# Convolution pieces woven into an attention kernel: two free streams over all chunks in place of streams in pairs

## The chip, the cores and the metric

The kernel runs on one core of a Trainium2 chip. The core has a matrix engine (TensorE, PE in the rows), a vector engine (VectorE, DVE), an activation engine (ScalarE, ACT), a general engine (GpSimd, POOL) and an engine that issues most transfers (SyncE, SP). Each engine takes its instructions strictly in the order in which the program lists them and waits on semaphores for the others. The metric is the time of one execution in microseconds (us); lower is better. Three runs of the kernel before took 1151.06 to 1153.36 us.

## The reference

Two independent computations share the launch. Their results stand side by side in the output.

```python
# A: a long convolution, 2048 positions, 576 channels, 128 states per channel
P = exp(dt * A[:, :, None] * l)                   # A, B, C complex
K = einsum("dn,dnl,dn->dl", C, P, dt * B).real    # kernel of the convolution
y = irfft(rfft(u, 2L) * rfft(K, 2L))[:L] + u * Dskip
# B: attention, 2048 positions, 32 query heads of 18, one shared key and value head
q = x @ wq ; k = x @ wk ; v = x @ wv
p = softmax(q k^T * 18 ** -0.5)
out = (p v) @ wo
return concatenate([y, out])
```

## The kernel before

**Attention.** Keys lie on partitions, so a score tile is 128 keys by 2 heads by 512 queries. There are 1,024 of them. For each, PE makes two matmuls (`s`, L516), ACT one exponential into a tile `P` (L527), and PE multiplies by the values into the bank `ops` (L823; one product takes the `P` of two score tiles, 512 products in all). Score tiles have three buffers in PSUM. The order is written in rounds (L835): a round writes the scores of three tiles, then fills PE until a score buffer is free again with products and with pieces of other work. There are 342 rounds. Every 16 products DVE copies `ops` to `o` (L534), and PE may write the one `ops` bank again only after that copy. Beside it run the query projections (`q`), bounds on the scores (`up`) and the output projection (`op`, 40 pieces of four matmuls for each 512 queries). What is left of the last output projection is done after the last product, in `finish` (L625, tiles `fin`).

**Convolution.** 576 channels are worked on in 12 chunks of 48. A chunk has a `front` (L1264): DVE makes powers of the states' exponentials (`factors`, rows `t`, `fr`, `sum`, `dif`) and two tables (`tables`, rows `tab`, `tt`), from which PE makes the kernel (`kg`, four banks a chunk, copied by DVE to `ksb`); it then goes through DRAM into the tile `kt`. Its `back` (L1337): PE transforms the input `u` (banks `hu`, `lu`, evacuated by DVE into `scu`) and the kernel (`hk`, `lk` into `sck`), DVE multiplies (`ks`, `acc`, `pt`, `sv`, `w`), and PE transforms back (`iy`). At chunks 0, 1, 5 and 9 `powers` makes the exponentials and sines for the chunks up to the next of these, a burst: ACT loads another table, does two sines, and loads the exponential's table again. A stream that comes to the burst yields "b" (L1124) and is let go once 8 units of attention's own PE work wait beside it or 16 steps have passed.

All of these pieces on PE (`kg`, `hu`, `lu`, `hk`, `lk`, `iy`, `q`, `up`, `op`) share one PSUM bank (`bank`, L221): the next can begin only when DVE has evacuated the one before.

**What sets the order.** The program is written by a planner in Python with a running guess of when each engine is free (`Clock`). Work other than scores and products lies in generators (`Stream`) that yield "p" before a piece for PE, "v" before a piece for DVE, "w" to wait. `Conv.go` (L1448) advances one conv stream by one piece whenever `fill` (L785) asks; among streams that can go it takes the one that has had the least vector work. `RATE` and `PACE` tie the conv's vector work to the steps of attention (a step is one product): while the conv is behind `PACE` per step, attention's side pieces stand back (L796). `turn` (L1439) puts the streams up in pairs: `back(k)` beside `front(k + 1)`, and the next pair only when both have ended. `meanwhile` (L1287) puts conv vector rows in front of an evacuation while the guess says that the vector engine would stand idle.

```python
if self.n < NCK and not any(st.live for st in self.streams):
    self.n += 1
    self.streams = [Stream(self.back(k, self.kt), self.k)]
    if k + 1 < NCK:
        self.streams.append(Stream(self.front(k + 1), self.k))
```

Of the kernel before, what the change touches and what calls it, by code (L numbers as in the profile page):

```python
# [47 lines left out]
PACE = 1.79  # L48
# [4 lines left out]
GAP = 0.4  # L53
DEFER = 0.5
# [9 lines left out]
NCK = D // ND  # L64
# [918 lines left out]
class Conv:  # L983
# [21 lines left out]
    def setup(self):  # L1005
        nc, cp, a = self.nc, self.cp, self.a
        self.raw, self.stored = {}, 0.0
        self.ut, self.ut_ready, self.kt = {}, [0.0, 0.0], None
        self.dft = cp.tile([P, 2048], F32, name="dft_sb")
        self.pos = cp.tile([P, 2, NB], F32, name="pos_sb")  # L1010
        self.hp = cp.tile([P, 1], F32, name="hp_sb")
        nc.vector.memset(self.hp, HALF_PI)
# [251 lines left out]
    def front(self, k):  # L1264
# [20 lines left out]
        self.kt, self.kt_ready = kt, self.k.t + 9.0  # L1285
# [51 lines left out]
    def back(self, k, kt):  # L1337
# [7 lines left out]
        tt(us[:, 0:4, :], us[:, 4:8, :], us[:, 8:12, :], op=ALU.add)  # L1345
        ks = p1.tile([P, 12, NE], F32, tag="ks", name=f"ks{k}")
# [73 lines left out]
    def early(self):  # L1420
        nc = self.nc
        nc.scalar.dma_start(self.pos, self.a["pos"])
        self.load_burst(0)
        self.load(0)
        self.n, self.burst = -1, False
        self.streams = [Stream(self.front(0), self.k)]
# [12 lines left out]
    def turn(self):  # L1439

        if self.n < NCK and not any(st.live for st in self.streams):
            self.n += 1
            k = self.n
            self.streams = [Stream(self.back(k, self.kt), self.k)] if k < NCK else []
            if k + 1 < NCK:
                self.streams.append(Stream(self.front(k + 1), self.k))

    def go(self, step, credit, lock):  # L1448
        self.turn()
# [4 lines left out]
        for st in self.streams:  # L1454

            if st.kind == "b":
                if st.asked < 0:
                    st.asked = step
                if self.beside() >= 8 or step > st.asked + 16 or self.n < 0:
                    st.kind, st.asked = "v", -1  # L1460
        for st in sorted(self.streams, key=lambda st: (not st.holds, st.work)):
            w0, st.ahead = self.k.work, ahead
            if st.go(step, credit, lock):
                self.work += self.k.work - w0
# [6 lines left out]
    def drain(self):  # L1471
        while self.streams:
            for st in sorted(self.streams, key=lambda st: (not st.holds, st.work)):
# [3 lines left out]
            self.turn()  # L1477
# [98 lines left out]
```

## Time and profile before

| what | value |
|---|---|
| median of 3 runs | 1151.15 us |
| lowest, highest run | 1151.06, 1153.36 us |
| profiled execution, first to last instruction | 1153.0 us |
| PE busy | 1083.5 us, 94% |
| ACT busy | 998.8 us, 87% |
| DVE busy | 987.4 us, 86% |
| POOL busy | 140.6 us, 12% |
| granted TensorE clock, mean | 0.99 |

The profile is one execution. No time of it is known beside its span, which lies between the lowest and the highest run. Busy time of PE counts modelled ends of matmuls that overlap, so 94% is not 94% of what PE could do. In the rows each single-precision matmul shows as two records, so that "x16" of a piece such as `lu` are 8 matmuls, and a piece of four matmuls is "x8". In the order below the count is of matmuls.

### The profile page before, as it was taken

How to read it: one execution, taken by the hardware profiler on the slowest of the kernel's cores; microseconds unless marked ns; L12 is line 12 of the kernel's file. 1: busy time of each engine (PE TensorE's matmuls, PEld its weight loads, DVE VectorE, ACT ScalarE, POOL GpSimd, SP SyncE). 2: the span in 40 equal slices, each digit the busy share in tenths (PEclk: the TensorE clock that was granted, in tenths of full speed). 3: DMA queues.
4: the chain of work that ended last, by engine and by line, in shares of the span. 5: the costliest groups of instructions: out<-in, count | busy, mean ns of one | idle time of the engine just before them, and what ended most of it. 6: DMA issues, size and time to landing. Idle time of an engine off the chain costs nothing.

```text
span 1153.0 us, 33012 instructions
## 1 busy us (share of the span) xinstructions
PE 1083.5 (94%) x13886; PEld 395.9 (34%) x13886; DVE 987.4 (86%) x1679; ACT 998.8 (87%) x1052; POOL 140.6 (12%) x257
## 2 busy tenths in 40 slices
PE   6999899989999999989999999999998999999998
PEld 2333233333333334323333333333332333332423
DVE  3697997998997897897799899898699799799694
ACT  2888979879989898998998899988999988899891
POOL 5232320112032000001021200001040000000000
PEclk9899999999999999999999999999999999999999
DMA  7422242114122202112222300202221301301201
GB/s 224 130 57 84 76 133 89 45 41 135 32 67 78 74 29 88 45 63 93 82 79 71 110 21 28 93 28 85 75 78 46 111 20 39 106 19 54 77 33 58
DMA packets 59279, 83.37 MB, mean 72 GB/s; under 512 B 14867, under 2 KB 35335, under 8 KB 58613
## 3 DMA queue, kind: packets, MB, share of 16 engines
q1 hardware_dynamic: 47557, 73.24, 19.4%
q0 software_dynamic: 10848, 7.37, 2.6%
q8 instruction: 111, 1.82, 0.6%
q10 hardware_dynamic: 720, 0.58, 0.2%
q14 instruction: 43, 0.35, 0.1%
HBM read 46.59 MB, written 33.85 MB: 70 GB/s over the span
## 4 chain that ended last, share of the span: by engine, by line
PE 64%; DVE 15%; ACT 14%; issue 5%; DMA 1%; SPq 0%; ACTq 0%; DVEq 0%
PE ops L823 27%; PE s L516 17%; ACT P L527 12%; PE op L193 5%; PE q L408 3%; DVE tab L119 3%; PE kg L1257 3%; PE iy L193 3%; DVE ks L119 1%; DVE acc L119 1%; DVE t L119 1%; PE hk L193 1%; PE fin L193 1%; PE lk L193 1%; DMA xr<-xT 1%
## 5 line engine op out<-in xcount | busy, mean ns | idle before, releaser
L527 ACT ACTIVATE P<-s 128x1024 f32<-128x1024 f32 x992 | 934.8, 1034 | 104.6 <-PE s L516 102.2
L823 PE MATMUL ops<-P,v_sb 128*32 128x512 f32 x4096 | 513.0, 601 | 8.5 <-DVE o L123 8.4
L516 PE MATMUL s<-aug,kaug 55*128 55x512 f16 x2048 | 309.9, 384 | 36.6 <-ACT P L527 30.7
L516 PEld LDWEIGHTS <-kaug 55*128 55x128 f16 x2048 | 92.2, 94 | 371.7 <-issue 328.5
L823 PEld LDWEIGHTS ops<-P,v_sb 128*32 128x32 f32 x4096 | 117.2, 110 | 162.6 <-issue 126.1
L458 POOL DMA_DIRECT2D qd<-qh x116 | 65.7, 573 | 323.2 <-DVE qh L127 320.6
L408 PE MATMUL q<-x,wq_sb 128*32 128x256 f32 x1360 | 84.2, 382 | 3.2 <-DVE sck L119 2.5
L193 PE MATMUL op<-wo_sb,oT 126*32 126x288 f32 (+1 forms) x1048 | 74.8, 410 | 2.6 <-DVE sck L119 1.2
L119 DVE TENSOR_TENSOR tab<-tab,tt 128x576 f32<-128x576 f32 (+1 forms) x72 | 59.1, 821 | 1.4
L123 DVE COPY ksb<-kg 128x192 f32<-128x192 f32 x48 | 17.5, 364 | 49.1 <-PE kg L1257 48.9
L119 DVE TENSOR_TENSOR tt<-fr,sum 128x576 f32<-128x576 f32 (+1 forms) x72 | 58.9, 818 | 0.0
L119 DVE TENSOR_TENSOR tab<-tab 128x576 f32<-128x576 f32 (+1 forms) x72 | 58.9, 818 | 0.0
L119 DVE TENSOR_TENSOR tab<-fr,dif 128x576 f32<-128x576 f32 (+1 forms) x72 | 58.9, 818 | 0.0
L119 DVE TENSOR_TENSOR tab<-sum,fr 128x576 f32<-128x576 f32 (+1 forms) x72 | 58.8, 816 | 0.0
L408 PEld LDWEIGHTS q<-x,wq_sb 128*32 128x32 f32 x1360 | 40.5, 110 | 43.4 <-issue 19.1
L1168 POOL MEMSET fr<- 128x192 f32 x24 | 9.8, 494 | 323.8 <-DVE tt L119 225.2
L119 DVE TENSOR_TENSOR acc<-acc,pt 128x1728 f32<-128x1728 f32 (+2 forms) x36 | 48.7, 1352 | 0.3
L119 DVE TENSOR_TENSOR pt<-us,ks 128x1728 f32<-128x1728 f32 (+2 forms) x36 | 48.2, 1351 | 0.0
L525 ACT ACTIVATE P<-s,bias 128x1024 f32<-128x1024 f32 x32 | 32.7, 1131 | 15.1 <-PE s L516 15.1
L193 PEld LDWEIGHTS op<-wo_sb,oT 126*32 126x32 f32 (+1 forms) x1048 | 29.8, 110 | 42.2 <-issue 17.4
L1257 PEld LDWEIGHTS kg<-tab 128*32 128x32 f32 x2304 | 35.5, 110 | 22.9 <-issue 7.9
L1257 PE MATMUL kg<-tab 128*32 128x64 f32 x2304 | 41.8, 221 | 1.5 <-DVE ksb L123 1.1
(160 smaller groups left out, 1018.0 us busy)
## 6 DMA issues: line engine op xcount, KB each, us to landing
od<-o SPq DMA_DIRECT2D x31, 256.0 KB
aug<-qd SPq DMA_DIRECT2D x124, 55.0 KB
u<-u SPq DMA_DIRECT2D x12, 384.0 KB
kd<-ksb SPq DMA_DIRECT2D x12, 384.0 KB
kt<-kd SPq DMA_DIRECT2D x48, 96.0 KB
outa<-u SPq DMA_DIRECT2D x12, 384.0 KB
pw<-pw SPq DMA_DIRECT2D x8, 528.0 KB
oT<-od SPq DMA_DIRECT2D x16, 252.0 KB
```

The source lines that it names most:

```text
L119: return self.v.tensor_tensor(out, *a, **k)
L123: return self.v.tensor_copy(out, *a, **k)
L193: nc.tensor.matmul(ps[j:e], w[:, j:e], x, start=start, stop=stop, tile_position=(0, j))
L408: nc.tensor.matmul(ps[o, 256 * f:256 * f + 256], w[:, k, i], xt[:, k, x], start=(k == 0), stop=(k == 4), tile_position=(0, 32 * j))
L458: q.dma_start(qd[h:h + n, row + d:row + d + nd, cs], src[i1:i1 + n * nd, :cs.stop - cs.start])
L516: nc.tensor.matmul(ps[:, j, :], self.kaug[r, kb * P:(kb + 1) * P], t[r, :], start=True, stop=True)
L525: nc.scalar.activation(pt, ps, AF.Exp, bias=self.bias, scale=SCALE / QQ)
L527: nc.scalar.activation(pt, ps, AF.Exp, scale=SCALE / QQ)
L823: nc.tensor.matmul(o_ps[32 * j:32 * j + 32, :], self.v[:, kb, :], pts[2 * n + j // 2][:, j % 2, :], start=(kb == 0), stop=(kb == 15), tile ...
L1168: nc.gpsimd.memset(t[:, :, 0:NF:8], one)
L1257: nc.tensor.matmul(ps[32 * g:32 * g + 32, d, :], t[:, :32], t[:, 32:], start=(j == 0), stop=(j == 1), tile_position=(0, 32 * g))
```

## The change

The pairs go. One stream runs all 12 fronts, another all 12 backs. `begun` holds the last chunk whose kernel has been sent to `kt`. A back of chunk 0 waits for kernel 0; a back of chunk k may begin, with the transform of its input, once kernel k - 1 has been sent (`LAG`), and waits before the transform of its kernel until kernel k has been sent. A front waits with its store into `kt` until the back before it has read the tile, as it did. Among streams whose next piece is a vector piece, `go` now takes the stream that had the last vector piece (`on`) first. `PACE` falls from 1.79 to 1.75. The burst's test looks at `begun`. No arithmetic changes.

```diff
-PACE = 1.79
+PACE = 1.75
...
+LAG = (0, -1)
...
-        self.kt, self.kt_ready = kt, self.k.t + 9.0
+        self.kt, self.kt_ready, self.begun = kt, self.k.t + 9.0, k
...
-    def back(self, k, kt):
+    def back(self, k):
...
         yield from self.transform(lambda r: ut[:, r, :], us[:, 4:12, :], f"u{k}", self.ut_ready[k % 2])
         yield "v", 0.0, False
         tt(us[:, 0:4, :], us[:, 4:8, :], us[:, 8:12, :], op=ALU.add)
+        while self.begun < k:
+            yield "w", 0.0, False
+        kt = self.kt
         ks = p1.tile([P, 12, NE], F32, tag="ks", name=f"ks{k}")
...
-        self.n, self.burst = -1, False
-        self.streams = [Stream(self.front(0), self.k)]
+        self.burst, self.on = False, None
+        self.streams = [Stream(self.fronts(), self.k), Stream(self.backs(), self.k)]
+
+    def fronts(self):
+        for k in range(NCK):
+            yield from self.front(k)
+
+    def backs(self):
+        for k in range(NCK):
+            while self.begun < LAG[k > 0] + k:
+                yield "w", 0.0, False
+            yield from self.back(k)
...
-    def turn(self):
-
-        if self.n < NCK and not any(st.live for st in self.streams):
-            self.n += 1
-            k = self.n
-            self.streams = [Stream(self.back(k, self.kt), self.k)] if k < NCK else []
-            if k + 1 < NCK:
-                self.streams.append(Stream(self.front(k + 1), self.k))
-
     def go(self, step, credit, lock):
-        self.turn()
...
-                if self.beside() >= 8 or step > st.asked + 16 or self.n < 0:
+                if self.beside() >= 8 or step > st.asked + 16 or self.begun < 0:
                     st.kind, st.asked = "v", -1
-        for st in sorted(self.streams, key=lambda st: (not st.holds, st.work)):
+        for st in sorted(self.streams, key=lambda st: (not st.holds, st.kind == "v" and st is not self.on, st.work)):
             w0, st.ahead = self.k.work, ahead
+            kind = st.kind
             if st.go(step, credit, lock):
+                if kind == "v":
+                    self.on = st
                 self.work += self.k.work - w0
                 return True
```

Line numbers of the kernel after are higher by one from L54 on (by more behind the changed functions). Three places show how the order moves.

DVE at the transform of the input of chunk 9 (`scu9`), before. `fr10`, `t1_10` and `t2_10` belong to the front of chunk 10.

```order
L123 COPY scu9_11647<-hu90_11663 128x384
L123 COPY fr10_11677<-pw_10_11557 128x48x4 x2
L123 COPY fr10_11677<-pw_10_11557 128x48x3
L123 COPY fr10_11677<-pw_10_11557 128x48x4 x2
L123 COPY fr10_11677<-pw_10_11557 128x48x3
L119 TENSOR_TENSOR t1_10_11691<-pw_10_11557 128x48x4
L119 TENSOR_TENSOR t2_10_11692<-pw_10_11557 128x48x4
L119 TENSOR_TENSOR fr10_11677<-t1_10_11691,t2_10_11692 128x48x4
L119 TENSOR_TENSOR t1_10_11691<-pw_10_11557 128x48x4
L119 TENSOR_TENSOR t2_10_11692<-pw_10_11557 128x48x4
L119 TENSOR_TENSOR fr10_11677<-t1_10_11691,t2_10_11692 128x48x4
L119 TENSOR_TENSOR scu9_11647<-lu90_11686,scu9_11647 128x384
```

The same place after. `stage3` is a burst's row, of the front.

```order
L124 COPY scu9_11036<-hu90_11037 128x384
L120 TENSOR_TENSOR scu9_11036<-lu90_11047,scu9_11036 128x384
L120 TENSOR_TENSOR scu9_11036<-lu90_11047,scu9_11036 128x2x192
L120 TENSOR_TENSOR stage3_10387<-stage3_10387,m3_10388 128x792 x2
L124 COPY scu9_11036<-hu91_11064 128x384
L120 TENSOR_TENSOR stage3_10387<-stage3_10387,m3_10388 128x792 x2
L120 TENSOR_TENSOR scu9_11036<-lu91_11094,scu9_11036 128x384 x2
```

Ten lines (twelve instructions) of the other stream stood between the copy of `hu90` and the first row that frees `lu90`. None stands there now, and two rows of the front stand on either side of the copy of `hu91`.

DVE where the first table of chunk 7 is done (`tab7_0`) and its kernel bank is copied (`ksb7`), before; `acc6` and `ks6` belong to the back of chunk 6.

```order
L119 TENSOR_TENSOR tab7_0_8582<-tab7_0_8582 128x24x24
L119 TENSOR_TENSOR tab7_0_8582<-tab7_0_8582,tt7_0_8_4_8838 128x24x24
L119 TENSOR_TENSOR acc6_8697<-acc6_8697,pt6_2_8850 128x96x6
L119 TENSOR_TENSOR acc6_8697<-acc6_8697 128x768
L123 COPY ksb7_8581<-kg7_0_0_8921 128x4x16x3
```

The same place after.

```order
L120 TENSOR_TENSOR tab7_0_8420<-tab7_0_8420 128x24x24
L120 TENSOR_TENSOR tab7_0_8420<-tab7_0_8420,tt7_0_8_4_8572 128x24x24
L120 TENSOR_TENSOR ks6_8219<-sck6_8220 128x2x192 x4
L124 COPY ks6_8219<-ks6_8219 128x32x6
L120 TENSOR_TENSOR ks6_8219<-ks6_8219 128x32x18
L124 COPY ksb7_8419<-kg7_0_0_8643 128x4x16x3
```

Two rows of the back stood between the last table row and the copy; six stand there now (one line is four rows).

PE at the end, before: from the last matmul of the last score tile (`s3_15_15`) over both halves of the last transform back (`iy110`, `iy111`) and the last products (`ops3_7`) to the first tiles of `finish` (`fin0`, `fin1`) and its broadcast `bc`.

```order
L516 MATMUL s3_15_15_14227<-aug3_113,kaug_109 128x512
L193 MATMUL iy110_14232<-w11_14162,dft_sb_98 32x192 x16
L823 MATMUL ops3_7_13960<-P3_14_14_14203,v_sb_115 32x512 x2
L823 MATMUL ops3_7_13960<-P3_15_14_14205,v_sb_115 32x512 x2
L823 MATMUL ops3_7_13960<-P3_14_15_14207,v_sb_115 32x512 x2
L823 MATMUL ops3_7_13960<-P3_15_15_14230,v_sb_115 32x512 x2
L193 MATMUL iy111_14258<-w11_14162,dft_sb_98 32x192 x16
L193 MATMUL fin0_14281<-wo_sb_107,oT3_13187 32x288 x16
L193 MATMUL fin1_14282<-wo_sb_107,oT3_13187 32x288 x8
L669 MATMUL bc_14280<-rc_last_14279,b4_13989 128x256
```

The same place after.

```order
L517 MATMUL s3_15_15_14277<-aug3_113,kaug_109 128x512
L194 MATMUL iy111_14282<-w11_14169,dft_sb_98 32x192 x16
L824 MATMUL ops3_7_14001<-P3_14_13_14222,v_sb_115 32x512 x2
L824 MATMUL ops3_7_14001<-P3_15_13_14224,v_sb_115 32x512 x2
L824 MATMUL ops3_7_14001<-P3_14_14_14249,v_sb_115 32x512 x2
L824 MATMUL ops3_7_14001<-P3_15_14_14251,v_sb_115 32x512 x2
L824 MATMUL ops3_7_14001<-P3_14_15_14253,v_sb_115 32x512 x2
L824 MATMUL ops3_7_14001<-P3_15_15_14280,v_sb_115 32x512 x2
L194 MATMUL fin0_14317<-wo_sb_107,oT3_13146 32x288 x12
L194 MATMUL fin1_14318<-wo_sb_107,oT3_13146 32x288 x8
L670 MATMUL bc_14316<-rc_last_14315,b4_13974 128x256
```

The first half (`iy110`) has moved ahead of the last score tile, the second half ahead of the last three products, and 20 matmuls of `fin` come before `bc` where there were 24. Over the whole of `finish` there are 92 where there were 116: six pieces of the output projection moved into the rounds, which hold 131 of them before and 137 after.

## Rows read from the trace of the kernel before


**Rows 1.** the page, parts 1 and 4: busy us (share) xinstructions; the chain by engine

```profile
PE 1083.5 (94%) x13886; PEld 395.9 (34%) x13886; DVE 987.4 (86%) x1679; ACT 998.8 (87%) x1052; POOL 140.6 (12%) x257
...
PE 64%; DVE 15%; ACT 14%; issue 5%; DMA 1%; SPq 0%; ACTq 0%; DVEq 0%
```

**Rows 2.** the view of waits: engine, line, waited for: us in total, times, longest

```profile
ACT P L527 <- PE s L516: 102.2, 186, 2.4
...
DVE ksb L123 <- PE kg L1257: 48.9, 33, 2.9
PE s L516 <- ACT P L527: 30.7, 81, 2.0
...
PEld lu L193 <- DVE scu L123: 11.0, 16, 1.1
...
PEld kg L1257 <- DVE ksb L123: 7.1, 11, 1.1
```

**Rows 3.** timeline of PE, 917 to 932 us: start us, us, engine line op, [idle before]

```profile
918.24 0.86 PE L193 MATMUL lu<-u,dft_sb 128*32 128x192 f32 x16
...
930.88 1.18 PE L193 MATMUL op<-wo_sb,oT 126*32 126x288 f32 x16 [0.81 <-DVE scu L119]
```

**Rows 4.** timeline of DVE, the same stretch

```profile
919.09 0.61 DVE L119 TENSOR_TENSOR t<-pw 128x192 f32<-128x192 f32 x2
919.74 0.52 DVE L119 TENSOR_TENSOR fr<-t,t 128x192 f32<-128x192 f32 x1
...
921.31 1.01 DVE L119 TENSOR_TENSOR scu<-lu,scu 128x384 f32<-128x384 f32 x2
...
929.71 1.02 DVE L119 TENSOR_TENSOR scu<-lu,scu 128x384 f32<-128x384 f32 x2
```

**Rows 5.** groups by line: form xcount | busy us, mean ns of one | idle before

```profile
L119 DVE TENSOR_TENSOR t<-pw 128x192 f32<-128x192 f32 x36 | 11.2, 355 | 0.3
```

**Rows 6.** timeline of all engines, 118 to 147 us, the first burst

```profile
132.42 1.28 ACT L1125 ACT_TABLE_LOAD   x1
...
133.06 4.09 PE L408 MATMUL q<-x,wq_sb 128*32 128x256 f32 x72
...
137.64 1.28 ACT L527 ACT_TABLE_LOAD   x1
...
140.01 0.60 PE L516 MATMUL s<-aug,kaug 55*128 55x512 f16 x2 [2.00 <-ACT P L527]
```

**Rows 7.** timeline of all engines, 244 to 262 us

```profile
250.92 0.69 DVE L123 COPY o<-ops 128x512 f32<-128x512 f32 x1
...
251.66 1.07 PE L823 MATMUL ops<-P,v_sb 128*32 128x512 f32 x8 [2.26 <-DVE o L123]
```

**Rows 8.** table of windows; PEclk is the granted clock, 1 is 2.4 GHz

```profile
140.00:146.00 6.00, 5.37 (x24) 0.94 (x25) 6.00 (x9) 4.54 (x5) 2.41 (x6) 0.51 0.45 141
146.00:150.00 4.00, 3.23 (x34) 0.82 (x30) 3.83 (x15) 2.85 (x3) 0.91 (x3) 0.89 0.93 265
...
250.00:254.00 4.00, 2.34 (x14) 0.43 (x14) 4.00 (x6) 1.58 (x3) 2.69 (x5) 0.84 0.45 126
254.00:258.00 4.00, 4.00 (x70) 1.61 (x70) 2.59 (x5) 2.21 (x3) 0.00 (x0) 0.73 0.25 85
```

**Rows 9.** timeline of PE from 1126 us to the end

```profile
1126.76 0.39 PE L516 MATMUL s<-aug,kaug 55*128 55x512 f16 x2
...
1130.12 1.48 PE L193 MATMUL iy<-w,dft_sb 128*32 128x192 f32 x32
1131.41 3.10 PE L193 MATMUL fin<-wo_sb,oT 126*32 126x288 f32 x48
...
1135.14 4.57 PE L193 MATMUL fin<-wo_sb,oT 126*32 126x288 f32 x72
...
1145.26 2.15 PE L193 MATMUL fin<-w,o_last 128*32 128x288 f32 x32
```

**Rows 10.** timeline of ACT, 1120 to 1153 us

```profile
1121.18 5.61 ACT L527 ACTIVATE P<-s 128x1024 f32<-128x1024 f32 x6 [0.46 <-PE s L516]
```

More of the change, by code (lines that the diff above doesn't have):

```diff
@@ L1006, in setup @@
         nc, cp, a = self.nc, self.cp, self.a
-        self.raw, self.stored = {}, 0.0
+        self.raw, self.stored, self.begun = {}, 0.0, -1
         self.ut, self.ut_ready, self.kt = {}, [0.0, 0.0], None
@@ L1471, in drain @@
     def drain(self):
-        while self.streams:
-            for st in sorted(self.streams, key=lambda st: (not st.holds, st.work)):
+        while any(st.live for st in self.streams):
+            for st in sorted(self.streams, key=lambda st: (not st.holds, st.kind == "w", st.work)):
                 if st.live:
@@ L1476, in drain @@
                     break
-            self.turn()
 def build(tc, **aps):
```

## The prediction

> **What bounds the kernel now.** I read the page first. PE is busy for 1083.5 us of the 1153.0 us span, ACT for 998.8, DVE for 987.4, and the chain that ended last runs over PE for 64%, DVE for 15% and ACT for 14% [rows 1]. The reader is to see that no engine has much to spare, and that PE leads. The view of waits comes next. ACT waits for scores from PE for 102.2 us in 186 places of at most 2.4 us each, and PE waits for ACT to free a score buffer for 30.7 us [rows 2]. So the loop of 342 rounds is a hand-over between these two, with PE late more often than ACT. What the change moves is work of the third engine, DVE. It can reach the time only where PE waits for DVE: in the one bank that all smaller pieces share, and in the one bank of the products. The timelines show both, and I read them last, with the end of the kernel.
>
> Three places matter. First, in the transform of an input: `lu` of chunk 9 starts at 918.24 and runs 0.86 us [rows 3], so it is done at 919.10, but its evacuation starts at 921.31, because vector rows of the next chunk's front stand before it [rows 4]. The second `lu` there is cleared only from 929.71 on [rows 4], and PE stands for 0.81 us before the next piece [rows 3]. Second, two stops of 2 us or more: 2.00 us after the first burst [rows 6], and 2.26 us where PE waits for the copy `o` that starts at 250.92 [rows 7]. Behind each, the granted clock is 0.51 over 140 to 146 us and 0.84 and 0.73 over 250 to 258 us [rows 8], that is, partly at 1.2 GHz in place of 2.4. Third, the end: from 1126.76 to 1147.41 PE works without a stop on the last score, `iy`, `ops` and `fin` [rows 9].
>
> **The change part by part.** The sum is made against the profiled 1153.0 us, and the difference is carried over to the median, which lies 1.85 us lower. Instruction counts on DVE and PE hardly change: by the order DVE has 1,685 rows for 1,679, six additions for the six output pieces that go from `finish` into the rounds.
>
> *The end.* By the order `finish` loses six pieces of four matmuls, out of the stretch where PE has no stop. From 1131.41, before `bc`, six pieces take 3.10 us by their row, and from 1135.14 nine take 4.57 [rows 9], about 0.5 us each: 6 × 0.5 = 3.0 us. Ahead of it both `iy` halves and one product change places with the last score. The PE work behind the last group of three scores falls by one `op` piece, which is done earlier, 0.5 us. Part of the 3.0 could be lost if `bc` waits for DVE instead: `rc_last` no longer stands behind the addition of the last `iy`, so I see no cause. **−3.4 us**, bounds −3.5 and 0.
>
> *The same six pieces in the rounds.* Late rounds already hold one such piece each, and there ACT runs six exponentials and then waits 0.46 us [rows 10], 0.23 us a round. That is all that PE costs there: 6 × 0.23 = 1.4. The bounds are 0 and the full PE time of six pieces, 3.1 us. **+1.4.**
>
> *Evacuations of `hu` and `lu`.* Over 12 chunks, 156 vector instructions of other work stand between the first copy of `hu` and the last row on `lu` in the order before, and 77 after. With their durations from the trace that is 78 and 51 us, a third less. PE's weight loads wait 11.0 us for `scu` now [rows 2]. A third of it goes: **−3.8**, bounds −11.0 and 0. What is late next there is the score hand-over.
>
> *Evacuation of the kernel banks.* With a back always at hand, 161 instructions stand between a last table row and the first copy of `kg`, where 59 did, and 33 for 26 between the two copies: 58 us more by the same durations. The cover is DVE's own wait for `kg`, 48.9 us now [rows 2]. 9.4 us are left uncovered. Queued behind each such copy is the next user of the bank, where PE waits 7.1 us now [rows 2]. Of DVE's time 15% is on the chain [rows 1]: **+1.4**, bounds 0 and +9.4.
>
> *Sticking to a stream.* The order changes stream 276 times on DVE where it did 434 times. So more rows read what the row just before them wrote: 521 for 442. Two independent rows `t<-pw` of 355 ns each [rows 5] take 0.61 us together, so the second starts 0.10 before the first ends; `fr<-t,t`, which reads them, starts 0.04 us after their end [rows 4]. That is 0.14 us for each such pair, 79 × 0.14 = 11.1 us more DVE time. At 15% on the chain: **+1.7**, bounds 0 and +11.1.
>
> The Trainium skill, "VectorE: DVE Perf Modes", section "The DRAIN you can't avoid", says that the next vector instruction does not start until the pipe of the one before has emptied, with or without a semaphore between them (it leaves some cases to another section). By that rule neighbours that depend on each other cost no more than others, and this term would be 0 and the sum 1.7 us lower. The trace has the 0.14 us between the two kinds, so I keep the term.
>
> *The two stops.* The one at 251 us costs 2.26 us plus what the low clock takes: 0.16 × 4 and 0.27 × 4 = 1.7 us of PE speed [rows 7, 8], together 4.0. The cause is that nothing stands on PE between the last product of one group and the first of the next; after, a `kg` bank of 24 matmuls stands there. It goes. The one after the first burst costs 2.00 us plus 0.49 × 6 and 0.11 × 4 = 3.4 [rows 6, 8], together 5.4. There ACT is away from 132.42 to 138.92 [rows 6] and PE has 4.09 us of `q` [rows 6] and a product. After, the burst meets `iy`, `hu` and `lu` pieces with evacuations between them, of about the same length, and I leave this stop as it is. **−4.0**, bounds −9.4 and +10.8 (two more such stops, at the other two bursts, which have none now).
>
> `PACE` and the start conditions move pieces and add none. The transfers are the same; on SP, the entries of `kd` and `kt` move past a few others, and they land beside vector work of the other stream, of which there is now always some. I count nothing for them; if that work ran out, a back would wait for its kernel as it does now.
>
> Sum: −3.4 + 1.4 − 3.8 + 1.4 + 1.7 − 4.0 = −6.7 us: 1146.3 for the profiled span, **1144.5 us** for the median.
>
> **The rivals.**
>
> *Only the end is gained.* The loop is held by the score hand-over (102.2 us of ACT's waits and 30.7 of PE's [rows 2]), and late evacuations are absorbed in it: the waits for `scu` and `ksb` are in weight loads and of 1.1 us at most [rows 2]. Then −3.4 + 1.4 = −2.0: 1149.2 us. Against it: the stop of 2.26 us is no hand-over.
>
> *Slower: the bursts lose their cover.* Before, the burst meets 9 or 10 ready pieces of `q` or `op` within two banks. After, by the order, 10 to 18 rounds lie between its first exponential and its sines (24 to 36, 133 to 143, 243 to 256; before 25 to 31, 135 to 136, 247 to 247), so the front waits out the 16 steps, and the pieces on PE are `iy`, `hu`, `lu`, five banks that each need an evacuation. If PE then stands for 2 us at each of the three, every one costs 5.4 us, two of them new: 10.8 on top of −6.7 gives +4.1, 1155.3 us. It decides from the point where PE has done its pieces before ACT is back, 6.5 us after it left.
>
> *Slower: DVE becomes the bound.* If DVE's idle time no longer covers anything, the 9.4 and 11.1 us count in full, nothing is gained on `scu` or `o`: −2.0 + 20.5 = +18.5, 1169.7 us. Against it: DVE is busy for 86% [rows 1].
>
> *More is gained.* Both stops and all of the 11.0 us go: −3.4 + 1.4 − 11.0 + 1.4 + 1.7 − 9.4 = −19.3, 1131.9 us.
>
> That the change doesn't do what it says I leave out: the order shows `hu` of chunk 1 ahead of that chunk's first `kg`, and the fewer changes of stream.
>
> **How the numbers follow.** Forecast 0.50, with a range of its own of 1138 to 1149; only the end 0.20; bursts 0.13; DVE 0.07; more 0.10. A measurement tells about 0.2%, 2.3 us, from no change. The forecast is faster in 0.48 and the same in 0.02; the second case splits 0.02, 0.16, 0.02; the next two are slower, the last faster: faster 0.60, same 0.18, slower 0.22. The range 1132 to 1158 takes in the burst rival and reaches the larger gain; it leaves out the DVE rival, half of the last, and tails.
>
> **What would show it.** Right: the last `fin` ends nearer to the last exponential by some 3 us; no stop of 2 us at a copy `o` near 250 us; PE's weight loads wait under 8 us for `scu`; DVE waits under 15 us for `kg`; DVE's busy time grows by about 10 us. Wrong: new stretches of granted clock near 0.5 behind the bursts, or PE's waits for `ksb` grown well past 7 us. The forecast fails if ACT's wait for scores has not fallen from 102.2 us by at least 3 us.

## The result and the profile after

The kernel after takes 1157.45 us (median of 8 runs, 1153.88 to 1160.50) and the kernel before 1151.57 beside it: a ratio of 1.0043 with a 95% interval of 1.0028 to 1.0059. It is slower by some 5 us (the medians lie 5.9 apart), where the prediction said 7 us faster. The profiled execution took 1158.27, with a span of 1156.5 us, 3.5 more than before.

The page of the kernel after, parts 1 and 4, answers to [rows 1]:

```profile
PE 1081.2 (93%) x13886; PEld 390.0 (34%) x13886; DVE 995.2 (86%) x1685; ACT 999.4 (86%) x1052; POOL 139.7 (12%) x257
...
PE 59%; DVE 24%; ACT 10%; issue 5%; DMA 1%; SPq 1%; DVEq 0%; ACTq 0%
```

PE works 2.3 us less and yet the span is longer: PE stands more. DVE has gone from 15% to 24% of the chain. The view of waits of the kernel after (engine, line, waited for: us in total, times, longest) answers to [rows 2]:

```profile
ACT P L528 <- PE s L517: 110.1, 186, 4.9
...
PE s L517 <- ACT P L528: 29.7, 84, 0.5
DVE ksb L124 <- PE kg L1258: 19.7, 18, 2.9
...
PEld lu L194 <- DVE scu L124: 12.4, 16, 1.1
...
PE ops L824 <- DVE o L124: 11.1, 14, 1.3
...
PEld kg L1258 <- DVE ksb L124: 7.2, 11, 1.9
...
PE kg L1258 <- DVE ql L132: 2.4, 2, 1.8
...
PE iy L194 <- DVE ql L132: 1.6, 1, 1.6
...
PE lu L194 <- DVE scu L124: 1.4, 2, 0.7
PE hu L194 <- DVE u L120: 1.4, 2, 0.7
PE hk L194 <- DVE ql L132: 1.4, 2, 1.1
PE iy L194 <- DVE u L120: 1.3, 2, 0.7
...
PE hu L194 <- DVE scu L120: 1.1, 3, 0.4
```

ACT waits longer for scores (110.1 for 102.2 us), so the forecast's own test fails. `ql` is the last row that clears a `q` bank, `u` the row that clears an `iy` bank. The longest wait of PE for a score buffer is 0.5 us for 2.0: the stop behind the first burst is gone.

The end went as forecast. PE from the last scores on, answering to [rows 9]:

```profile
1133.59 0.39 PE L517 MATMUL s<-aug,kaug 55*128 55x512 f16 x2
1133.91 1.51 PE L194 MATMUL iy<-w,dft_sb 128*32 128x192 f32 x32
1135.23 2.76 PE L824 MATMUL ops<-P,v_sb 128*32 128x512 f32 x24
1137.81 2.61 PE L194 MATMUL fin<-wo_sb,oT 126*32 126x288 f32 x40
...
1141.02 3.12 PE L194 MATMUL fin<-wo_sb,oT 126*32 126x288 f32 x48
...
1148.71 2.15 PE L194 MATMUL fin<-w,o_last 128*32 128x288 f32 x32
```

From the start of the last score to the end of the last `fin` it is 17.27 us (1150.86 - 1133.59), and 20.65 before (1147.41 - 1126.76): 3.4 us less. But the last score comes 6.8 us later. So the question is the loop.

Where PE stands, by the timeline of PE in the kernel after, three stretches:

```profile
148.97 1.51 PE L194 MATMUL iy<-w,dft_sb 128*32 128x192 f32 x32 [0.68 <-DVE u L120]
151.16 0.86 PE L194 MATMUL hu<-u,dft_sb 128*32 128x192 f32 x16 [0.68 <-DVE u L120]
152.70 0.86 PE L194 MATMUL lu<-u,dft_sb 128*32 128x192 f32 x16 [0.68 <-DVE scu L124]
...
529.19 1.88 PE L824 MATMUL ops<-P,v_sb 128*32 128x512 f32 x8 [1.07 <-DVE o L124]
...
602.05 0.88 PE L1258 MATMUL kg<-tab 128*32 128x64 f32 x48 [1.84 <-DVE ql L132]
603.47 1.06 PE L824 MATMUL ops<-P,v_sb 128*32 128x512 f32 x8 [0.55 <-DVE o L124]
```

And DVE of the kernel after, beside the first and the last of them:

```profile
148.37 0.55 DVE L120 TENSOR_TENSOR u<-u,iy 128x384 f32<-128x384 f32 x1 [2.31 <-PE iy L194]
...
598.04 2.53 DVE L120 TENSOR_TENSOR ks<-ks 128x576 f32<-128x576 f32 x3
600.49 0.68 DVE L128 TENSOR_SCALAR qh<-q 128x512 f16<-128x512 f32 x1
601.21 0.69 DVE L132 SCALAR_TENSOR_TENSOR ql<-q,qh 128x512 f16<-128x512 f32 x1
```

The reader is to see two kinds of stop. At 148.97 DVE stood idle for 2.31 us and took the bank as soon as it was full: 0.07 us after the last matmul the evacuation starts, it takes 0.55, and PE goes on 0.05 later, 0.68 in all. I call this a **prompt** stop: PE has nothing to put between two users of the one bank, and no reordering on DVE can help. At 602.05 the evacuation of `q` is **late**: rows of `ks` stand before it (three of them shown).

I add up every stop of PE that DVE ends, from 40 us after the start to the last score. Before it is 18.6 us in 26 places, of which 5.9 are prompt (the evacuation starts within 0.35 us) and 12.8 late; after 26.5 in 37 places, 11.2 prompt and 15.3 late. (Some rows that end a stop clear no bank; putting them on the other side moves up to 1 us between the two, and leaves the sums.) That is +7.9 us. Four more items belong to the account. PE's waits for ACT are 1.2 lower there. The scores run 2.1 ahead at 40 us (the 13th tile starts at 39.80 us for 41.88). Six pieces of 0.5 us more stand on PE (+3.0). And the low clock takes 1.7 us of PE speed, by the windows below, where its two stretches before took 3.4 and 1.7 [rows 8] (-3.4). The sum is +4.2 of the 6.8; for the other 2.6 us I have no row.

The granted clock of the kernel after, in the windows of [rows 8] and in three new ones:

```profile
140.00:146.00 6.00, 4.66 (x44) 1.15 (x46) 5.93 (x12) 4.48 (x6) 3.49 (x6) 1.00 0.62 173
...
146.00:150.00 4.00, 3.32 (x70) 1.78 (x66) 0.61 (x2) 3.97 (x3) 0.00 (x0) 1.00 0.09 25
150.00:154.00 4.00, 2.65 (x52) 1.33 (x48) 1.49 (x3) 3.97 (x4) 0.00 (x0) 1.00 0.26 102
...
250.00:254.00 4.00, 3.81 (x36) 0.95 (x32) 4.00 (x5) 3.75 (x5) 0.00 (x0) 1.00 0.36 82
254.00:258.00 4.00, 3.35 (x30) 0.71 (x22) 3.93 (x3) 4.00 (x6) 0.00 (x0) 1.00 0.10 39
528.00:532.00 4.00, 2.93 (x33) 0.47 (x18) 3.93 (x10) 1.61 (x3) 1.01 (x1) 0.66 0.18 67
532.00:536.00 4.00, 4.00 (x58) 1.66 (x58) 3.97 (x6) 3.26 (x4) 0.00 (x0) 0.91 0.26 65
```

Both stretches of low clock of the kernel before are gone (140 and 252 us), and a new one lies behind the stop at 529 us: (0.34 + 0.09) x 4 = 1.7 us of PE speed.

### The profile page after: what moved, and what is told of

Same layout as the page of the kernel before. It is cut to its first block, busy times and chain, and to the rows that moved or that the text cites. A ratio compares the mean times of both kernels' runs of the same rounds, so it can differ in the third digit from the quotient of the medians.

```text
span 1156.5 us, 33032 instructions
## 1 busy us (share of the span) xinstructions
PE 1081.2 (93%) x13886; PEld 390.0 (34%) x13886; DVE 995.2 (86%) x1685; ACT 999.4 (86%) x1052; POOL 139.7 (12%) x257
## 4 chain that ended last, share of the span: by engine, by line
PE 59%; DVE 24%; ACT 10%; issue 5%; DMA 1%; SPq 1%; DVEq 0%; ACTq 0%
PE ops L824 24%; PE s L517 15%; ACT P L528 9%; PE op L194 5%; PE q L409 3%; DVE tab L120 3%; PE iy L194 3%; DVE t L120 3%; PE kg L1258 2%; DVE fr L120 2%; DVE acc L120 2%; DVE ks L120 2%; PE hk L194 1%; PE lu L194 1%; DVE stage L120 1%
## 5 line engine op out<-in xcount | busy, mean ns | idle before, releaser
L528 ACT ACTIVATE P<-s 128x1024 f32<-128x1024 f32 x992 | 935.9, 1033 | 112.7 <-PE s L517 110.1
L824 PE MATMUL ops<-P,v_sb 128*32 128x512 f32 x4096 | 509.2, 597 | 11.2 <-DVE o L124 11.1
L194 PE MATMUL op<-wo_sb,oT 126*32 126x288 f32 (+1 forms) x1096 | 78.5, 410 | 0.9 <-DVE ob L124 0.9
L120 DVE TENSOR_TENSOR tab<-tab 128x576 f32<-128x576 f32 (+1 forms) x72 | 58.7, 816 | 0.0
L526 ACT ACTIVATE P<-s,bias 128x1024 f32<-128x1024 f32 x32 | 32.6, 1137 | 11.2 <-PE s L517 11.2
L120 DVE TENSOR_TENSOR ks<-ks 128x576 f32<-128x576 f32 (+1 forms) x48 | 41.0, 854 | 0.8
```

The costliest lines, as they stand in the source:

```text
L120: return self.v.tensor_tensor(out, *a, **k)
L194: nc.tensor.matmul(ps[j:e], w[:, j:e], x, start=start, stop=stop, tile_position=(0, j))
L526: nc.scalar.activation(pt, ps, AF.Exp, bias=self.bias, scale=SCALE / QQ)
L528: nc.scalar.activation(pt, ps, AF.Exp, scale=SCALE / QQ)
L824: nc.tensor.matmul(o_ps[32 * j:32 * j + 32, :], self.v[:, kb, :], pts[2 * n + j // 2][:, j % 2, :], start=(kb == 0), stop=(kb == 15), tile ...
```

## The experiments

Three theories at the start. **T1**: sticking queues long runs of one stream in front of attention's own evacuations. **T2**: the bursts wait out their steps and meet a chain of pieces in one bank. **T3**: the constants of the planner were chosen for one order, and any other order lands some us away. In the tables, "last score" (its end) and "behind it" (span less last score) come from the profiled execution, "PE for DVE" is the sum above, prompt + late.

### One part of the change at a time

The first two kernels are the kernel after with the sort key of before; `free_only` also has PACE 1.79. `pairs_stick` is the kernel before with the new key, `after_b0` is the kernel after and lets a burst come at once.

```diff
-        for st in sorted(self.streams, key=lambda st: (not st.holds, st.kind == "v" and st is not self.on, st.work)):
+        for st in sorted(self.streams, key=lambda st: (not st.holds, st.work)):
...
-                if self.beside() >= 8 or step > st.asked + 16 or self.begun < 0:
+                if True or step > st.asked + 16 or self.begun < 0:
```

> The kernel after without the sticking of vector work: two free streams, PACE 1.75, but the vector rows again go to the stream with the least work done. T1 (sticking queues long runs of one stream's vector rows ahead of attention's own evacuations): the lateness summed over the evacuations of q, up, ops and kg falls back from 54.1 us in the kernel after towards the 31.9 of before, PE's waits for the copy o from 11.1 towards 8.4, and the time comes to 1148 to 1152 us. T2 (the loss is at the three bursts, which come through the free streams): the time stays at 1156 to 1158, with three losses of 2 to 3 us each still at the rounds of the bursts. T3 (any other order of the pieces scatters by some 5 us): anything from 1147 to 1158, with no relation to the lateness.

> Two free streams alone: no sticking, and PACE 1.79 as before. T1: like free_pace, 1148 to 1152 us. T2: 1156 to 1158 us, the bursts still wait out their 16 steps (the order has them 9, 1 and 11 rounds after their first exponential, for 12, 10 and 13 in the kernel after), the second burst, 1 round, is the one that would cost nothing. T3: as far from free_pace as from the kernel before, though only PACE differs.

> The kernel before with the sticking alone: the streams still run in pairs, PACE 1.79. T1: slower than before by 3 to 6 us (1154 to 1158), with the lateness of q, up, ops and kg above the 31.9 us of before. T2: no slower than before (1150 to 1153), since the bursts come 12, 1 and 1 rounds after their first exponential and pieces of the back still wait for them. T3: 1147 to 1157, with no relation to the lateness.

> The kernel after, in which a burst does not wait until eight pieces of other work stand ready or 16 steps have gone, but comes at once (1 round after its first exponential, in all three places). T2: the losses behind rounds 143 and 256 go, 4 to 6 us less than the kernel after: 1152 to 1154. T1: the same as the kernel after within 2 us (1156 to 1159), the lateness of q, up, ops and kg stays near 54 us; a burst that comes with nothing beside it can cost 2 us each in PE stops instead. T3: 1150 to 1160, with losses in other places.

| kernel | median us | ratio to before, 95% | last score | behind it | PE for DVE |
|---|---|---|---|---|---|
| before | 1152.69 | | 1127.1 | 25.9 | 5.9 + 12.8 |
| after | 1157.45 | 1.0028 to 1.0059 | 1134.0 | 22.5 | 11.2 + 15.3 |
| free_pace | 1205.32 | 1.0444 to 1.0489 | 1141.5 | 62.0 | 13.3 + 17.0 |
| free_only | 1201.87 | 1.0416 to 1.0453 | 1147.5 | 51.7 | 10.6 + 23.4 |
| pairs_stick | 1173.63 | 1.0172 to 1.0209 | 1137.5 | 34.2 | 7.1 + 18.6 |
| after_b0 | 1204.35 | 1.0431 to 1.0473 | 1137.2 | 62.9 | 14.2 + 10.8 |

All four missed their numbers. In pairs sticking does cost, 21 us, as T1 has it by sign; in the free streams it saves some 45, so it is not what the change loses, and T1 falls. Nor is the burst's waiting: T2 falls as put. Each of these kernels is one order, so the figures are no prices of a rule. Most of the loss stands behind the last score, where PE of `free_pace` shows:

```profile
1154.49 1.45 PE L194 MATMUL lk<-kt,dft_sb 128*32 128x192 f32 x16 [0.67 <-DVE sck L124]
1177.69 2.79 PE L194 MATMUL iy<-w,dft_sb 128*32 128x192 f32 x32 [21.76 <-DVE w L120]
```

The convolution is not done when attention ends. By the order, `kg` of its last chunk is issued in steps 501 to 512 of 512 there, and in 466 to 488 in the kernel after (472 to 488 before). What is left is one chain with nothing beside it, 21.76 us of vector work in it. This can be read from the order alone. In the loop, too, each of the four comes 10 to 20 us later to the last score than before, and each has 6 to 15 us more of PE's waits for DVE.

### Is it DVE's load?

Both kernels with three quarters of the work of the 360 rows `tab` and `tt` left out (and `kg` reading what is written); the order on PE, DVE, ACT and POOL is unchanged.

```diff
-        tt = V.tensor_tensor
         n = ND // NSB
+
+        def tt(out, x, y, op):
+            self.k.dve(out, 1.04e-3, x, y)
+            nc.vector.tensor_tensor(out[:, :n // 4], x[:, :n // 4], y[:, :n // 4], op=op)
...
-                        t = self.tab[:, j, g * TB + ds.start + d, :]
+                        t = self.tab[:, j, ds.start + d, :]
```

> The kernel before with three quarters of the table's work left out: the 360 rows tab and tt work on 6 of the 24 columns, and kg reads those alone; the order on PE, DVE, ACT and POOL stays as it is, row by row. DVE is then busy for about 210 us less. It shows how much of the loop PE owes to DVE. T1' (the loop's time follows PE's waits for DVE, 18.6 us in the kernel before): these waits fall to some 8 us, the last score ends 8 to 11 us earlier than 1127, the time is 1140 to 1145. Rival (the order on PE itself sets the loop, in the hand-over of scores with ACT): the waits go over to ACT, and the time stays within 3 us of the kernel before.

> The kernel after with the same three quarters of the table's work left out, and its own order on the four engines. T1' (what the loop lost, 6.8 us to the last score, is vector work that stands in front of evacuations): PE's waits for DVE, 26.5 us in the kernel after, fall to the same few us as in the shortened kernel before, the last scores of the two end within 2 us of each other, and this kernel is the faster of the two by the 3.3 us of its end. Rival (the order of the pieces on PE costs the 6.8 us, whatever DVE does): the last score is still 5 to 8 us later than in the shortened kernel before, and the time 2 to 5 us longer.

The times are 1146.73 (0.9937 to 0.9973 of before) and 1152.15 us (0.9975 to 1.0012). DVE is busy for 812.0 and 820.7 us, 175 less, and that is worth 5.6 and 5.3 us: DVE's load as such is not the bound. PE's waits for DVE fall from 18.6 to 15.1 us and from 26.5 to 21.0, not to the 8 us that was expected. The kernel after stays 5.4 us slower, its last score at 1127.8 for 1119.1, and the first theory falls again. PE's waits for DVE in the shortened kernel after:

```profile
PE ops L824 <- DVE o L124: 9.3, 13, 1.3
...
PE iy L194 <- DVE ql L132: 1.6, 1, 1.6
PE lu L194 <- DVE scu L124: 1.4, 2, 0.7
PE hu L194 <- DVE u L120: 1.4, 2, 0.7
PE iy L194 <- DVE u L120: 1.3, 2, 0.7
```

In the shortened kernel before, `ops` waits for `o` 7.1 us in 7 places, and `iy` for nothing. The late waits of the two are now equal, 8.8 and 8.9 us; the prompt ones are 6.3 and 12.1. So in this pair 5.8 of the 8.7 us to the last score go with prompt stops, that is, with how the pieces stand on PE. That the rest does too isn't shown. Of the two expectations for this kernel the second came nearer, with 8.7 us for its 5 to 8.

### What a piece costs in a round

The kernel after, with its 17 output pieces of the last column issued behind the loop; they keep their place in the planner's account. What else follows from that (a copy in place of the last addition, the planner's list of open pieces) is left out of the cut.

```diff
-                ps = self.bank(288, f"op{c}_{t}_{n}_{ms[0]}")
+                K.pe(0.0, K.fill)
                 for m in ms:
-                    matmul4(nc, ps, o[:126, m, t * P:(t + 1) * P], self.wo[:126, m, cs], start=(m == ms[0]), stop=(m == ms[-1]))
                     K.pe(0.485)
...
-                    self.rest.discard((t, n, m))
+                    self.owed.discard((t, n, m))
                 self.conv.meanwhile()
-                if ms[0] == 0:
-                    V.tensor_copy(part[:, t, cs], ps)
-                else:
-                    V.tensor_tensor(part[:, t, cs], part[:, t, cs], ps, op=ALU.add)
+                K.dve(part[:, t, cs], 1.04e-3, part)
...
```

> The kernel after, in which the 17 output pieces of the last column (68 fin matmuls) that it does in late rounds are issued behind the loop instead: fin grows from 92 to 160, all other work keeps its order. 17 x 0.49 us = 8.3 us of PE work move from rounds to the end. Price theory of the prediction (a piece costs 0.23 us in a round and 0.5 at the end): the last score comes 3.9 us earlier, the end takes 8.3 longer, 4.4 us slower than the kernel after, 1162. Rival (PE is the bound in those rounds too, so a piece costs the same 0.49 in either place, and moving six of them gains nothing): the last score comes 7 to 8 us earlier, and the time stays within 1.5 us of the kernel after, 1156 to 1159.

1161.58 us (1.006 to 1.010), 4.1 more than the kernel after. The last score comes 2.8 us earlier (1131.18) and behind it stand 8.1 us more, with one `fin` group of:

```profile
1139.63 7.97 PE L194 MATMUL fin<-wo_sb,oT 126*32 126x288 f32 x128
```

So a piece costs 2.8 / 17 = 0.16 us in a round by the profile, 0.24 by the medians ((8.1 - 4.1) / 17), and 0.48 at the end. The prediction's prices, 0.23 and 0.5, hold for these 17 pieces. The rest of a piece would then fill time in which PE stood; that is inferred.

### The same rules with other constants

Nine kernels that differ from before or after in constants alone, which gives the same pieces another order (`free_stick` is after with PACE 1.79; "mix" is PACE 1.80, AHEAD 0.90 and DEFER 0.40 together; the names of the others have their value).

```diff
-PACE = 1.79
+PACE = 1.80
...
-AHEAD = 0.7
+AHEAD = 0.65
...
-DEFER = 0.5
+DEFER = 0.4
```

> The kernel before with its own rules and PACE 1.80 for 1.79: a hundredth of one constant gives another order, in which the convolution is done as early as before (kg of the last chunk in steps 471 to 488, hk and lk to 498) and 84 fin pieces are left for 116. It measures the scatter between orders that no rule tells apart. T3 (the constants were chosen for one order, and any other pays): 5 to 20 us slower than before in the loop, with PE's waits for DVE grown from 18.6 to 24 or more, less 4 us at the end. Rival (the rules of the change cost the time, not the reshuffling): within 3 us of before in the loop, and 1147 to 1152 us in all.

> The kernel after with PACE 1.79 as before: free streams and sticking together, one constant apart from the kernel after; the convolution is done as early (kg of the last chunk in steps 465 to 489, hk and lk to 498), and 96 fin pieces are left for 92. T3: as far from the kernel after as orders scatter, 1150 to 1166 us. Rival (free streams and sticking together have their own price, +5 us): 1155 to 1160, and PE's waits for DVE in the loop near the 26.5 us of the kernel after.

> The kernel before with AHEAD 0.65 for 0.70: vector work may be queued 0.05 us less ahead of PE. Another order of the same pieces by the same rules; the convolution is done as early (kg of the last chunk in steps 474 to 489, hk and lk to 498), and 96 fin pieces are left for 116. Scatter theory: it lands anywhere between 1146 and 1170 us, its sign not to be told from the constant, and its time follows PE's waits for DVE in the loop (18.6 us in the kernel before, 26.5 after, 23.4 with PACE 1.80) and the stretches of low clock. Rival (vector work queued ahead is what costs): 2 to 5 us faster than before.

> The kernel before with three constants changed (PACE 1.80, AHEAD 0.90, DEFER 0.40): the convolution is done earlier than in any order so far (kg of the last chunk in steps 470 to 482, the last iy in step 507 of 512), so that no iy piece stands behind the last score; 108 fin pieces are left. Scatter theory: 1145 to 1170, by PE's waits for DVE. Rival (the early end of the convolution is worth it): the end is 4 us shorter than before, and the time 1145 to 1150, faster than both kernels.

> The kernel after with DEFER 0.40 for 0.50, which moves products against scores: free streams, sticking and PACE 1.75 stay. The convolution is done as early as in the kernel after (kg of the last chunk in steps 466 to 490), 80 fin pieces are left for 92. Scatter theory: 1148 to 1165, as far from the kernel after as orders by the rules of before lie from before. Rival (free streams with sticking have a price of their own): 1155 to 1160, with PE's waits for DVE near 26.5 us.

> The kernel before with DEFER 0.40 for 0.50, the partner of the kernel after with the same constant (1150.95 us). The convolution is done early (kg of the last chunk in steps 468 to 483, the last iy in step 510), 100 fin pieces are left for 116. Scatter theory (no rule, but the one order that comes out, sets the time within some 10 us): 1148 to 1170, and the sign against its partner is open. Rival (free streams with sticking cost some 5 us at any constants): 1145 to 1147, 5 us below its partner.

> The kernel after with the three constants of the fastest kernel so far (PACE 1.80, AHEAD 0.90, DEFER 0.40), partner of the kernel before with the same three (1148.3 us). The convolution is done early (kg of the last chunk in steps 466 to 490, hk and lk to 498), 88 fin pieces are left for 92. Scatter theory: 1148 to 1165, since constants that suit the one set of rules say nothing on the other. Rival (free streams with sticking cost some 5 us): 1152 to 1155.

> The kernel after with AHEAD 0.65 for 0.70, partner of the kernel before with the same constant (1149.5 us). By its order the convolution is late: lu of the last chunk in step 507 of 512, hk and lk behind the last score, where the 22 us of vector work on its products then stand alone. Theory of the end (the end costs what is left of the convolution's chain): the last score comes within 8 us of the kernel after, the end takes 40 to 48 us, 1170 to 1185 in all. Rival (the streams catch up in the rounds, since PE has idle time there): 1150 to 1160.

> The kernel after with AHEAD 0.65 and DEFER 0.45; here the convolution is done early again (kg of the last chunk in steps 466 to 490, hk and lk to 498), and 80 fin pieces are left for 92. Scatter theory: 1146 to 1165; if it comes under 1150, the rules of the change reach the time that the rules of before reach with other constants (1148.3), and only the order tells the kernels apart. Rival (free streams with sticking cost some 5 us): not under 1152.

| kernel | median us | ratio to before, 95% | last score | behind it | PE for DVE | PE for ACT | low clock |
|---|---|---|---|---|---|---|---|
| before | 1152.1 | | 1127.1 | 25.9 | 5.9 + 12.8 | 31.7 | 5.7 |
| before_mix | 1148.30 | 0.9951 to 0.9982 | 1118.2 | 22.7 | 2.9 + 20.0 | 25.1 | 0.0 |
| before_ahead065 | 1149.47 | 0.9960 to 0.9986 | 1125.1 | 23.8 | 6.7 + 12.3 | 31.1 | 3.4 |
| before_defer04 | 1158.07 | 1.0034 to 1.0074 | 1133.8 | 22.5 | 4.5 + 17.7 | 35.0 | 3.4 |
| before_pace180 | 1169.41 | 1.0121 to 1.0165 | 1148.1 | 22.8 | 8.0 + 15.4 | 38.2 | 8.8 |
| after | 1157.45 | 1.0028 to 1.0059 | 1134.0 | 22.5 | 11.2 + 15.3 | 30.5 | 1.7 |
| after_defer04 | 1150.95 | 0.9978 to 1.0003 | 1127.3 | 21.5 | 11.1 + 11.2 | 27.5 | 1.7 |
| after_ahead065_defer045 | 1152.45 | 0.9992 to 1.0021 | 1127.3 | 21.5 | 10.4 + 11.3 | 28.3 | 1.7 |
| free_stick | 1157.08 | 1.0026 to 1.0059 | 1130.5 | 23.7 | 8.8 + 16.2 | 31.2 | 0.0 |
| after_mix | 1160.66 | 1.0047 to 1.0094 | 1136.1 | 22.5 | 7.7 + 18.3 | 30.7 | 3.4 |
| after_ahead065 | 1187.56 | 1.0281 to 1.0340 | 1135.0 | 49.5 | 11.1 + 15.9 | 31.2 | 2.1 |

"PE for ACT" is the same sum over stops that ACT ends, "low clock" is one less the granted clock, times its length, both from 40 us to the last score. The median of before is the mean of its five medians.

T3 holds in so far as another order lands some us away: a hundredth of PACE is worth 17 us under the rules of before. That the constants suit before's order best is not so, for two of its four neighbours are faster. And the ranges expected of the scatter are 15 to 25 us wide, so that meeting them says little.

With the constants as given the change is worth +5 us. With DEFER 0.40 on both sides it is -7.1, with the three of the mix +12.4, with PACE 1.79 (`free_stick`) +5, with AHEAD 0.65 +38. Its sign differs with the order. But the one pair in which it gains still has PACE 1.75 against 1.79. In the two pairs with all constants equal it costs 5 and 12 us. The rival, some 5 us at any constants, met `free_stick` (1155 to 1160) and is not ruled out by `after_ahead065_defer045` (not under 1152); it missed `after_defer04`, `before_defer04` and `after_mix`.

`after_ahead065` is the theory of the end once more: the last chunk's `lu` stands in step 507, and 49.5 us lie behind the last score. That one of the orders under after's rules, and none under before's, ends so late may belong to the rules; it was not tried.

With the convolution done in time there are five orders under each set of rules. Their mean is 1155.5 us under before's (1152.1, 1149.5, 1148.3, 1169.4, 1158.1) and 1155.7 under after's (1157.5, 1157.1, 1151.0, 1160.7, 1152.5). They are no random sample, and the late one is left out, but no price of the rules stands out of a scatter of 21 and 10 us. The waits do shift: prompt ones average 9.8 us under after's rules and 5.6 under before's, late ones 14.5 and 15.6.

PE's waits for DVE alone do not rank these ten. `before_mix`, the fastest, waits for DVE 4.3 us more than before, and its last score is 9.0 us earlier: PE waits 6.6 us less for ACT there, and no low clock falls in its loop. `before_pace180` waits 6.5 us more for ACT and loses 3.1 more to the clock. The three columns together rank the last scores without a miss under each set of rules: 48.0, 53.5, 56.0, 60.6 and 70.4 us for before's five, 51.6, 51.7, 56.2, 58.7 and 60.2 for after's, in the order of 1118.2 to 1148.1 and of 1127.3 to 1136.1. So an order is to be judged by all of PE's stops and the clock, and what sets them in an order is not shown.

`before_mix` and `before_ahead065` beat both kernels. PE of `before_mix` at the end:

```profile
1117.78 0.39 PE L516 MATMUL s<-aug,kaug 55*128 55x512 f16 x2
1118.10 0.69 PE L193 MATMUL op<-wo_sb,oT 126*32 126x288 f32 x8
1118.61 1.90 PE L823 MATMUL ops<-P,v_sb 128*32 128x512 f32 x16
1120.33 3.10 PE L193 MATMUL fin<-wo_sb,oT 126*32 126x288 f32 x48
```

No `iy` is left behind the last score. That execution was the shortest of its twelve (1142.70); the medians are 3.8 us apart.

## Why the prediction was wrong

*The end, -3.4:* right, 3.4 measured, and by the cause named: 24 fewer matmuls of `fin`.

*Six pieces in the rounds, +1.4:* borne out by `after_fin40`, 0.16 to 0.24 us each against 0.23.

*Evacuations of `hu` and `lu`, -3.8:* **this step failed.** What DVE does came as forecast: from the end of a group's matmuls to its evacuation, what exceeds 0.3 us added up to 27.6 us over the 48 `hu` and `lu` groups before and to 6.7 after. But PE had little to win there. The term took 11.0 us from weight loads [rows 2], and a weight load that waits does not hold PE while matmuls ahead of it still run: in 10.2 of these 11.0 us PE was busy. The same view of the kernel before, for PE's matmuls alone, has:

```profile
PE ops L823 <- DVE o L123: 8.4, 8, 2.3
...
PE q L408 <- DVE sck L119: 2.5, 2, 1.2
...
PE op L193 <- DVE sck L119: 1.2, 1, 1.2
...
PE lu L193 <- DVE scu L123: 0.8, 1, 0.8
PE op L193 <- DVE scu L119: 0.8, 1, 0.8
...
PE hu L193 <- DVE scu L119: 0.5, 1, 0.5
PE hk L193 <- DVE sck L119: 0.4, 1, 0.4
PE q L408 <- DVE scu L119: 0.4, 2, 0.2
```

For `scu` that is 2.5 us in all, the most that these stops of PE could give. After, PE's stops for `scu` are 1.4 us of `lu` and 1.1 of `hu`, again 2.5: the term came out as 0.0 for -3.8. The Trainium skill, "TensorE: Matmul & The Clock Gate", section "Architectural detail: the array is 16× 32×32, not 1× 128×128", says that PE's queue can pull weight loads ahead of matmuls in flight; the trace agrees, with 12.4 us of waiting weight loads of `lu` for `scu` after in 16 places, PE busy in 10.9 of them, and 1.4 us of `lu` matmuls in 2. (So "strictly in the order", as the first section has it for every engine, is too strong for PE's weight loads.) And "what is late next there is the score hand-over" was wrong: next was the bank itself. With the evacuation prompt, the next piece stands 0.68 us behind it, and the order after puts `iy`, `iy`, `hu`, `lu` there in a row.

What grew instead are for the most part stops that the sum has no term for. By the row that ended them, PE's stops for DVE go from nothing to 5.4 us for `ql` (the `q` bank) and from nothing to 2.7 for `u` (the `iy` bank), from 8.4 to 11.1 for `o`, and from 4.1 to 1.1 for `sck`. The prediction put `q` and `iy` at nothing without saying why.

*The two stops, -4.0:* the step named the stop at 251 us rightly, and it went, but the stop behind the first burst went too, against "I leave this stop as it is". Neither made up for stops in other places, as 1.07 us at 529 with low clock behind it and 2.4 at 602. The slower rival put 2 us and a low clock at each burst, two of them new. Prompt stops do lie there, at 149 to 153 us (2.0) and, by the same timeline, at 502 to 504 (2.3) and 870 to 874 (1.7). But they stand where other stops stood. In the 12 us from 2 us before ACT's first table load, PE's stops add up to 2.6, 2.3 and 2.2 us at the three bursts before, most of the last two for DVE, and to 2.0, 2.3 and 2.1 after. So the bursts cost PE no more than before, and over 146 to 154 us, with three stops of 0.68, the granted clock stayed 1.00.

*Kernel banks, +1.4:* PEld's waits for `ksb` are 7.2 for 7.1 us; late copies of `kg` did grow, by the sum above 0.3 us from 2.6 to 11.4, with PE's matmuls of `kg` waiting 3.6 us for 1.5. But 2.4 of the 3.6 are for `ql`, and PE's stops for `ksb` are 1.2 us for 1.1: the term was too high, and this cost is among the `ql` stops above. *Sticking, +1.7:* DVE is busy 7.8 us longer, 2.7 of it six more additions of 447 ns; the other 5.1 are under half of the 11.1 that bounded it. No run shows what they cost the span.

*The signs named:* no stop of 2 us near 250, the shorter end and the longer DVE held; the weight loads' 8 us for `scu` (12.4) and the 15 us of DVE for `kg` (19.7) did not.

So the sum for the loop, -3.3, came out as +6.8, and the largest part of it is PE's waits for DVE: forecast some 5 us lower (-3.8 - 2.3 + 1.4), measured 7.9 higher. Behind it lies a second fault, in the chances. The sum priced what the rules do on average, but a run shows one order, and the five orders by before's rules lie anywhere between 1148 and 1169 us. A gain of 7 us with 0.60 on faster was more than the rows could carry. What stays open: which property of an order makes its stops, for DVE and for ACT, and whether the rules have a mean price of a few us in either direction.

## What to carry to other kernels

When a planner orders the work, a changed rule is one draw among orders: here one set of rules spread over 21 us. Run the same rules with two or three neighbouring constants before the rule is judged, and compare the two sets at equal constants. Size a gain by the waits of the engine that bounds, here PE's matmuls, not by those of the weight loads that run ahead of it. Look for the stops that a new order puts up as well as for those that it takes away, and ask of each bank what stands between its two users once the evacuation is prompt. And look in the order for what is left behind the loop: a chain that ended alone cost 27 to 40 us here.

## What the runs showed of the hardware

- A hand-over of one bank from PE to DVE and back costs 0.68 us with DVE idle: 0.07 to the evacuation, 0.55 for 384 fp32 elements a partition, 0.05 to the next matmul.
- Stretches of low clock in the loop differ with the order: at 140 and 252 us before, one at 528 after, none in the profiled run of `free_stick`, and in that of `before_pace180` five places (148, 256, 324, 480, 856). Of the eight runs of the kernel after the shortest (1153.88) has a mean granted clock of 0.999 and the longest (1160.50) 0.993.
- Taking 175 us of work off DVE, busy for 86% of the span, brought 5.6 us of 1152.3 before and 5.3 of 1157.45 after.
- While weight loads of `lu` waited 11.0 us for DVE (before), PE's matmuls were busy for 10.2 of them.
